# A retention and gated-MLP kernel: the first MLP layer of blocks 4 to 8 by seven block products, with part of the gated product on GpSimd

## The chip, the cores and the metric

The kernel runs on one core of a Trainium2 chip. The metric is the device time of one execution in microseconds, the median over several runs. The engines are named as in the profile: PE is TensorE (PEld its weight loads), DVE is VectorE, ACT is ScalarE, POOL is GpSimd, SP is SyncE, which issues most DMAs.

## What is computed

For 8 batches, 8 heads, 576 positions and head size 64 the reference computes a retention (attention with a decay in place of a softmax), puts the heads side by side to 4608 tokens of 512 numbers, and sends them through an MLP with 2048 hidden units and the gate h·cos(h):

```python
scores = scale * np.matmul(q, k.transpose(0, 1, 3, 2))
Dmat = np.where(rel >= 0, gamma[:, None, None] ** rel[None, :, :], 0.0)
attn = np.matmul(scores * Dmat[None], v)
x = attn.transpose(0, 2, 1, 3).reshape(B * S, H * D)
h = x @ w_in            # 4608x512 by 512x2048
g = h * np.cos(h)
out = g @ w_out         # 4608x2048 by 2048x512
```

## The kernel before

The tokens are cut into nine MLP blocks of 512 tokens (`NTB`, j = 0 to 8), and the retention into 18 units of 256 positions of one batch (two of them gather the last 64 positions of four batches each). Two units make the 512 tokens of one block.

A unit: SP loads k, q and v in float32 into staging buffers (L463); POOL casts k (L454) and scales q and v by powers of the decay (L496) into bf16; k and q are transposed, for the first two blocks by PE (L517), later by DMA (L532). PE computes the scores in 64x64 tiles (`scores`, L565, all its matmuls recorded on L563), DVE masks them (L599), PE computes the outputs (`outputs`, L637): a `main` phase inside the chunks, a `fill` phase that adds k times v to the running states in PSUM (`states`, L612), and a `cross` phase with the states of earlier chunks, which waits for the end of `main` (`after` [0]). ACT copies the states (L631) and the unit's output into `xt` (L710, recorded on L453). The running states have two PSUM banks, `ST[0]` and `ST[1]`, for even and odd batches.

The first layer (`mlp1`, L727) makes 16 hidden tiles of 128 units for a block: four matmuls (L737) accumulate in one PSUM bank, ACT takes sin(h + pi/2) into `cb` (L745), and DVE multiplies PSUM by `cb` into `gt` (L748). In blocks 0 to 2 a tile is made in two halves of 256 tokens, in blocks 3 to 8 at once for 512.

The second layer is plain for block 0 (`plain2`, L767). For blocks 1 to 8 (`wino2`, L805) it is cut in two along tokens, hidden units and output columns, and made of seven block products in place of eight: DVE forms sums of `gt` quarters into `s` (L823, L829), PE makes 7x16 matmuls of 128x256 (L862) that accumulate in three banks, ACT copies three intermediate results into `sn` (L453), DVE adds them to the banks into `os` (L874). The sums of the weights (`tw`) are made once (`wsums`, L787).

The order of the work is written by a planner (`Graph.run`, L204): each task has a fixed duration, a due time (a period of 28.8 us for each block) and buffers from small rotating pools (`POOLS`, L315): six PSUM banks `bk`, three staging buffers each of k, q, v, three `cb`, three `sn`, three `os`. It simulates the five engines, an exclusive use of one SBUF port by DVE and POOL tasks that are marked `port`, the DMA, and PE's instruction fetches in steps of 256 (`FETCH`), and writes each engine's queue in the order of the simulated starts. Every queue then runs in that fixed order and waits on semaphores. Short matmuls on ones (L401) fill PE's gaps in the first microseconds.

Of the kernel before, what the change touches and what calls it, by code (L numbers as in the profile page):

```python
# [6 lines left out]
ALU = mybir.AluOpType  # L7
AF = mybir.ActivationFunctionType
F32 = mybir.dt.float32
# [120 lines left out]
class Graph:  # L130
# [3 lines left out]
    AHEAD, FETCH = 2000, 3000  # L134
# [44 lines left out]

    def first(self, t):  # L180
        need = {}
        for b in t.allocs:
            need[b.pool] = need.get(b.pool, 0) + 1
        return all(b in self.fifo[b.pool][:need[b.pool]] for b in t.allocs if b.pool in self.fifo)
# [19 lines left out]
    def run(self, dma_rate):  # L204
# [3 lines left out]
        left = [256, self.FETCH]  # L208
# [21 lines left out]
        def pick(e):  # L230
            cand = []
            for t in ready[e]:
# [4 lines left out]
                if e == "pe" and t.count > left[0]:  # L237
                    s = max(s, left[1] - t.dur * left[0] / t.count)
# [22 lines left out]
        while n < len(self.tasks):  # L261
# [10 lines left out]
            e = t.eng  # L272
            ready[e].remove(t)
# [5 lines left out]
            if e == "pe":  # L279
                if t.count > left[0]:  # L280
                    left[1] = s + t.dur * left[0] / t.count + self.FETCH
                    left[0] += 256
                left[0] -= t.count
# [9 lines left out]
            if t.dma is not None:  # L293
                dma_free = max(dma_free, s + (1700 if e == "pool" else 1150)) + t.dma
                done = dma_free + t.tail
# [18 lines left out]
class Kernel:  # L314
    POOLS = dict(bk=6, stgk=3, stgv=3, stgq=3, natk=3, natv=3, qnat=2, kt=3, qt=3, pt=4, sba=3, sbb=3, sbr=8, xt=2,  # L315
                 gt=2, s=9, cb=3, os=3, sn=3)
# [3 lines left out]
                cb=(TB, BF16), os=(1024, F32), sn=(TB, F32))  # L320
    FORDER = [0, 1, 2, 3, 8, 9, 10, 11, 4, 5, 6, 7, 12, 13, 14, 15]
    SPLIT = 2
    PLAIN = (0,)
    NOXBAR = {0, 1}
    PERIOD, T0, T1 = 28800, 14000, 30000

    def __init__(self, nc, es, q, k, v, w_in, w_out, out):
# [8 lines left out]
        self.TW = {n: sb(f"tw{n}", [128, 8 * 256], BF16) for n in (1, 2, 4)}  # L336
        self.WV = sb("wv", [128, 40], F32)
# [10 lines left out]
        self.ST = [nc.alloc_psum_tensor(f"st{i}", [128, 512], F32) for i in range(2)]  # L348
# [26 lines left out]
    def emit(self, order):  # L375
# [4 lines left out]
        for t in order:  # L380
            if t.eng == "pe":
                gap = t.start - warm
                if gap > 400 and self.wb.left:
                    self.warm(int((gap - 300) / 110 if not warm else 0.6 * (gap - 150) / 57))
# [126 lines left out]
    def tpe(self, src, off, rk, dst, wk, eng):  # L511
        bk = Buf("bk")

        def mm(e):
            tb = self.at(bk).ap().bitcast(BF16)
            for c in range(4):
# [5 lines left out]
                 alloc=() if self.first else (self.wb,), name="tpe", count=9)  # L522
# [17 lines left out]
    def emit_lanes(self, name, prio, phases, alloc=()):  # L540

        parts, t, n = [], 200, 0
        for lanes, reads, writes, after in phases:
# [7 lines left out]
            n += 2 * len(order) + 1  # L551
# [60 lines left out]
    def states(self, u, s, lanes, reads, writes):  # L612
        nk, nv = self.tiles[u]["natk"], self.tiles[u]["natv"]
        x = u[0] % 2
        for r in range(2):
            for c in range(4):
                for y in range(2):
                    i, o = 512 * y + (2 * c + r) * D, 512 * y + self.head(c, r) * D
                    lanes[s, r].append((64, self.mm(
                        lambda r=r, c=c: ap(self.ST[x], 512, 64 * r, 64, c * 64, [1, 64]),  # L620
                        lambda i=i: ap(self.at(nk), 1024, 64 * s, 64, i, [1, D]),
                        lambda o=o: ap(self.at(nv), 1024, 64 * s, 64, o, [1, D]),
                        start=u[1] == s == c == y == 0)))
        reads += [(t, y) for t in (nk, nv) for y in range(2)]
        writes.append(("st", x))
# [5 lines left out]
    def snap(self, u, s):  # L631
        b = self.sbd[u, s] = Buf("sba" if s == 0 else "sbr" if u[1] else "sbb")
        x = u[0] % 2
        self.copy("act", 280, lambda: self.at(b).ap(), lambda: ap(self.ST[x], 512, 0, 128, 0, [1, 256]),
                  [("st", x)], [(b,)], late=1000 if s == 0 else 3000)

    def outputs(self, u, prio, late):  # L637
# [5 lines left out]
        main, fill, cross = ({q: [] for q in self.LANES} for _ in range(3))  # L643
# [37 lines left out]

        for s in range(2):
# [3 lines left out]
        for s in range(2):  # L686
            for p in range(2):
                inter(s, p, 1 - s, cross)
# [5 lines left out]
        phases = [(main, reads, writes, [])]  # L694
        if late:
            phases.append((fill, [], [], []))
            for v, s in late:
                self.states(v, s, *phases[-1][:3])
        phases.append((cross, reads, writes, [0]))
# [27 lines left out]
    def mlp1(self, j, f, ses, prio):  # L727
# [7 lines left out]
        def mm(e):  # L735
            for c in range(4):
# [7 lines left out]
                 w=[(bk,)], alloc=[gt] + [self.wb] * (j == 1 and f == 0), prio=prio, name=f"m1_{j}_{f}", count=9)  # L744
# [8 lines left out]
    def store(self, j, half, os, cols=(0, DM)):  # L753
        c0, cn = cols[0], cols[1] - cols[0]
        if j < 8:
# [3 lines left out]
        for p0, n, b, r, step in parts:  # L759
# [4 lines left out]
                r=[(os, c) for c in range(2) if cols[0] <= 256 * c < cols[1]],  # L764
                sem=lambda p0=p0: f"o{os.slot}_{p0}_{c0}", dma=1550 * cn / DM * n / 128)

    def plain2(self, j, base, span):  # L767
        gt = self.gt[j]
        for half in range(2):
            os = Buf("os")  # L770
            for tt in range(2):
                bk = Buf("bk")
                for qd in range(4):
                    def mm(e, tt=tt, qd=qd, bk=bk, half=half):
                        for f in range(4 * qd, 4 * qd + 4):
# [6 lines left out]
                             + [("wout", qd, 0), ("wout", qd, 1)], w=[(bk,)], prio=base + span * i / 16, name=f"p2_{j}", count=9)  # L782
                self.copy("act", 490, lambda os=os, tt=tt: ap(self.at(os), 1024, 0, 128, 512 * tt, [1, 512]),
                          lambda bk=bk: self.at(bk).ap(), [(bk,)], [(os, 0 if tt == 0 else 1)])
# [20 lines left out]
    def wino2(self, j, base, span):  # L805

        gt = self.gt[j]
        S_ = {(i, q): Buf("s") for i in range(1, 5) for q in range(2)}
# [16 lines left out]
        for q in range(2):  # L825
            for i, x, y, r, op in (
                    (3, lambda q=q: a(0, 0, q), lambda q=q: a(0, 1, q), ak(0, 0, q) + ak(0, 1, q), ALU.subtract),
                    (4, lambda q=q: a(1, 0, q), lambda q=q: sv(2, q), ak(1, 0, q) + [(S_[2, q],)], ALU.subtract)):
                self.one("dve", 610, lambda e, i=i, q=q, x=x, y=y, op=op: e.tensor_tensor(sv(i, q), x(), y(), op),  # L829
                         r=r, w=[(S_[i, q],)], port=True, name=f"S{i}_{j}")  # L830
        A, Bb, C = Buf("bk"), Buf("bk"), Buf("bk")
# [12 lines left out]
        def right_t(i):  # L844
# [7 lines left out]
            7: (left_s(3), right_b(0, 1), lambda q: [(S_[3, q],), ("wout", q, 1)], A, False),  # L852
# [3 lines left out]
        for n, p in enumerate((1, 2, 6, 5, 7, 3, 4)):  # L856
            l, rr, keys, bank, first = spec[p]
            for q in range(2):
                def mm(e, l=l, rr=rr, bank=bank, first=first, q=q):
                    for f in range(4 * q, 4 * q + 4):  # L860
                        for tt in range(2):
# [139 lines left out]
```

## Time and profile before

| what | value |
|---|---|
| runs of the kernel before | 300.94, 302.74, 304.18 us; median 302.74 |
| the profiled execution | 301.62 us, of them 299.9 us span (first to last instruction) |
| granted TensorE clock | 1.000 |
| PE busy from 90 to 210 us | 120.0 of 120 us |
| DVE, ACT, POOL busy from 150 to 180 us | 22.54, 17.05, 13.12 us |
| last matmuls end, last ACT instruction ends | 295.74, 296.36 us |
| share of the 16 DMA engines, 120 to 150 us, 210 to 240 us | 1.04, 0.13 |

The profile is of one execution. Busy time counts from an instruction's start to its end, so that two pipelined instructions overlap: an instruction's duration is longer than the distance of two starts. The chain of waits is followed back from the last instruction: each piece is released by the one before it, so that its shares say what the end waited for. In a group's line stand the count, the busy time, the mean duration and the idle time in front of it with its releaser.

### The profile page before, as it was taken

Reading aid. Unit: us, or ns where it says so; the run is one execution under the profiler, and the core shown is the slowest. Engines: PE = TensorE matmul, PEld = TensorE weight load, DVE = VectorE, ACT = ScalarE, POOL = GpSimd, SP = SyncE. Lnnn points to the kernel's source line nnn. Section 1 sums busy time; section 2 is a strip of 40 time slices with the busy share of each in tenths; the row PEclk is TensorE's granted clock in tenths of the full one; section 3 lists DMA queues with packets and bytes.
Section 4 is the critical chain, followed back from the end, with each engine's and each line's share of the span. In section 5 each row is a group of like instructions: output and inputs, shape, how many; then the busy total and the mean of one; then the engine's idle time right before and its main releaser. Section 6 shows DMA issues by size and latency. Waiting matters only on the chain.

```text
span 299.9 us, 9086 instructions
## 1 busy us (share of the span) xinstructions
PE 285.2 (95%) x3809; PEld 202.7 (68%) x3815; DVE 213.0 (71%) x379; ACT 169.7 (57%) x315; POOL 101.4 (34%) x125
## 2 busy tenths in 40 slices
PE   6789888999999999999999999999999999999994
PEld 6667665666788876766676667666766666666683
DVE  2776495659985889697868686959777666667721
ACT  5369876556667565645655565466565555545420
POOL 3821960665825614825363515172100000000000
PEclk9999999999999999999999999999999999999999
DMA  7999789999999799997999986892103000300115
GB/s 199 252 203 274 202 129 236 280 200 299 207 251 297 151 194 281 214 227 210 229 280 232 244 188 94 194 236 53 24 2 140 2 2 2 140 2 0 70 73 140
DMA packets 101640, 49.87 MB, mean 166 GB/s; under 512 B 43488, under 2 KB 97248, under 8 KB 101600
## 3 DMA queue, kind: packets, MB, share of 16 engines
q1 hardware_dynamic: 97376, 45.10, 63.6%
q0 software_dynamic: 4224, 4.19, 8.8%
q8 instruction: 30, 0.49, 0.7%
q14 instruction: 10, 0.08, 0.1%
HBM read 36.70 MB, written 9.44 MB: 154 GB/s over the span
## 4 chain that ended last, share of the span: by engine, by line
PE 78%; DMA 14%; POOL 5%; issue 1%; SPq 0%; ACT 0%; DVE 0%; DVEq 0%
PE bk L737 35%; PE bk L862 33%; DMA stgq<-in_q_dram 8%; PE bk L563 6%; DMA wout<-in_moe_w_out_dram 3%; DMA win<-in_moe_w_in_dram 3%; PE bk L776 2%; POOL qnat L496 2%; POOL natv L496 2%; PE st L563 1%; POOL natk L454 1%; SPq L463 0%; POOL win L717 0%; POOL wout L721 0%; DVE qnat L496 0%
## 5 line engine op out<-in xcount | busy, mean ns | idle before, releaser
L745 ACT ACTIVATE cb<-bk,cpi 128x256 bf16<-128x256 f32 (+1 forms) x192 | 108.3, 583 | 82.0 <-PE bk L737 79.9
L737 PE MATMUL bk<-xt,win 128*128 128x256 bf16 (+1 forms) x768 | 144.2, 326 | 1.0 <-DMA win<-in_moe_w_in_dram 0.7
L748 DVE TENSOR_TENSOR gt<-bk,cb 128x256 bf16<-128x256 f32 (+1 forms) x192 | 103.8, 555 | 54.9 <-ACT cb L745 47.8
L737 PEld LDWEIGHTS bk<-xt,win 128*128 128x128 bf16 x768 | 72.3, 98 | 39.7 <-DVE pt L599 1.4
L496 POOL TENSOR_TENSOR natv<-stgv,wv 128x512 bf16<-128x512 f32 x36 | 37.7, 1070 | 37.0 <-PE bk L563 20.6
L599 DVE TENSOR_TENSOR pt<-bk,tr 128x512 bf16<-128x512 f32 x68 | 42.7, 682 | 5.5 <-PE bk L563 5.4
L496 POOL TENSOR_TENSOR qnat<-stgq,wq 128x512 bf16<-128x512 f32 x32 | 35.0, 1112 | 15.9 <-DMA stgq<-in_q_dram 15.3
L454 POOL CAST natk<-stgk 128x512 bf16<-128x512 f32 x34 | 21.3, 653 | 55.8 <-DMA stgk<-in_k_dram 44.8
L862 PE MATMUL bk<-wout,gt 128*128 128x256 bf16 x256 | 32.7, 273 | 0.0
L862 PE MATMUL bk<-tw,s 128*128 128x256 bf16 x256 | 32.7, 273 | 0.0
L862 PE MATMUL bk<-wout,s 128*128 128x256 bf16 x256 | 32.4, 273 | 0.0
L862 PEld LDWEIGHTS bk<-tw,s 128*128 128x128 bf16 x256 | 24.9, 98 | 8.1
L862 PEld LDWEIGHTS bk<-wout,gt 128*128 128x128 bf16 x256 | 24.7, 98 | 6.4
L862 PEld LDWEIGHTS bk<-wout,s 128*128 128x128 bf16 x256 | 24.7, 98 | 6.1
L453 ACT ACTIVATE xt<-bk 128x512 bf16<-128x512 f32 x36 | 23.5, 728 | 0.5 <-PE bk L563 0.5
L874 DVE TENSOR_TENSOR os<-bk,sn 128x512 f32<-128x512 f32 x24 | 16.4, 683 | 10.4 <-PE bk L862 10.4
L453 ACT ACTIVATE sn<-bk 128x512 f32<-128x512 f32 x24 | 14.3, 597 | 13.8 <-PE bk L862 13.8
L862 PE MATMUL bk<-tw,gt 128*128 128x256 bf16 x128 | 16.4, 273 | 0.0
L776 PE MATMUL bk<-wout,gt 128*128 128x512 bf16 x58 | 15.3, 380 | 0.6 <-issue 0.3
L862 PEld LDWEIGHTS bk<-tw,gt 128*128 128x128 bf16 x128 | 12.5, 98 | 4.0
L829 DVE TENSOR_TENSOR s<-gt 128x1024 bf16<-128x1024 bf16 x16 | 12.8, 800 | 0.2
L563 PE MATMUL bk<-qt,kt 64*64 64x128 bf16 (+1 forms) x576 | 12.1, 217 | 0.4 <-ACT xt L453 0.4
(58 smaller groups left out, 187.7 us busy)
## 6 DMA issues: line engine op xcount, KB each, us to landing
stgk<-in_k_dram SPq DMA_DIRECT2D x16, 512.0 KB, 7.0
stgq<-in_q_dram SPq DMA_DIRECT2D x16, 512.0 KB, 6.9
stgv<-in_v_dram SPq DMA_DIRECT2D x16, 512.0 KB, 6.9
out_dram<-os SPq DMA_DIRECT2D x16, 512.0 KB, 3.3
win<-in_moe_w_in_dram POOLq DMA_DIRECT2D x4, 512.0 KB, 9.0
wout<-in_moe_w_out_dram POOLq DMA_DIRECT2D x4, 512.0 KB, 10.0
stgk<-in_k_dram SPq DMA_DIRECT2D x8, 128.0 KB, 3.4
stgq<-in_q_dram SPq DMA_DIRECT2D x8, 128.0 KB, 3.5
```

Of the source, the lines that this page charges most:

```text
L453: return self.one(eng, dur, lambda e: e.activation(dst(), src(), AF.Copy), r=r, w=w, **kw)
L454: return self.one(eng, dur, lambda e: e.tensor_copy(dst(), src()), r=r, w=w, port=True, **kw)
L496: self.one(eng, 610 if eng == "dve" else 1000, lambda e, out=out, inp=inp, tab=tab, col=col, hs=hs: e.tensor_tensor(out(), inp(), ap(tab, ...
L563: return lambda e: e.matmul(out(), lhs(), rhs(), start=start, stop=True, skip_group_check=True)
L599: self.one("dve", 610, lambda e, r=r, b=b, pt=pt: e.tensor_tensor(ap(self.at(pt), 1024, 0, 128, 512 * r, [64 * ny * ny, 8 // ny // ny], [1 ...
L737: inst = e.matmul(ap(self.at(bk), 512, 0, 128, 0, [1, n]), ap(self.WIN, 4 * DFF, 0, 128, c * DFF + 128 * f, [1, 128]), ap(self.at(xt), 204 ...
L745: self.one("act", 70 + n, lambda e: e.activation(ap(self.at(cb), TB, 0, 128, 0, [1, n]), ap(self.at(bk), 512, 0, 128, 0, [1, n]), AF.Sin, ...
L748: self.one("dve", 75 + n / 0.96, lambda e: e.tensor_tensor(ap(self.at(gt), NF * TB, 0, 128, f * TB + 256 * h0, [1, n]), ap(self.at(bk), 51 ...
L776: inst = e.matmul(self.at(bk).ap(), ap(self.at(gt), NF * TB, 0, 128, f * TB + 256 * half + 128 * tt, [1, 128]), ap(self.WOUT, NF * DM, 0, ...
L829: self.one("dve", 610, lambda e, i=i, q=q, x=x, y=y, op=op: e.tensor_tensor(sv(i, q), x(), y(), op), r=r, w=[(S_[i, q],)], port=True, name ...
L862: inst = e.matmul(ap(self.at(bank), 512, 0, 128, 256 * tt, [1, 256]), l(f, tt), rr(f), start=(first and f == 0 and tt == 0), stop=True, sk ...
L874: self.one("dve", 610, lambda e: e.tensor_tensor(view(h, c), ap(self.at(bank), 512, 0, 128, 0, [256, 2], [1, 256]), ap(self.at(sn[name]), ...
```

## The change

Blocks 4 to 8 get their first layer by `seven1`, which works like `wino2`: for each of four groups g (two tiles of either half of the hidden units) PE makes seven products of four 128x256 matmuls into three banks, 112 matmuls for a block where there were 64 of 128x512. ACT copies three intermediate results per group into `sn`; DVE adds them to the banks into a new float32 buffer `h`; ACT takes the sine from `h`; POOL multiplies `h` by `cb` into `gt`. For the fourth quarter of a group the sine and the product (on DVE) read PSUM as before. `xsums` makes four sums of `xt` on DVE for each block, `wsums1` eight sums of `w_in` once.

With it come other edits. Both running states lie in one bank, cleared by a DVE memset for each batch, and `bk` has seven banks; `outputs` is cut into five phases in which the two row halves of PE never write the same bank, with three waits of PE for its own earlier phases in place of one. Staging goes from three buffers to two, `pt` from four to two, `s` from nine to six (one sum overwrites `gt`), `os` from three to two, `cb` and `sn` grow to four and five. The planner's fetch model, its counts and a DMA delay are new. The `w_out` loads wait for q of unit (1,1) where they waited for v, and unit (2,0) for the third `w_out` load where it waited for the second. In the last block bank A and its copies and stores are split by token half.

In the order of the queues after the change, PE has 240 matmuls more; POOL has 60 products more, between its conversions; SP's order is the same up to its 42nd instruction, with waits for POOL in more places. On POOL the four `w_out` loads stand ahead of the conversion of q of unit (1,1), behind which they stood. Thirteen units are converted, or are first in POOL's queue, when its first gated product comes.

```diff
-    POOLS = dict(bk=6, stgk=3, stgv=3, stgq=3, natk=3, natv=3, qnat=2, kt=3, qt=3, pt=4, sba=3, sbb=3, sbr=8, xt=2,
-                 gt=2, s=9, cb=3, os=3, sn=3)
+    POOLS = dict(bk=7, stgk=2, stgv=2, stgq=2, natk=3, natv=3, qnat=2, kt=3, qt=3, pt=2, sba=3, sbb=3, sbr=8, xt=2,
+                 gt=2, s=6, cb=4, os=2, sn=5, xs=3, h=4)
-    AHEAD, FETCH = 2000, 3000
+    AHEAD, FETCH = 2000, 6500
-        self.ST = [nc.alloc_psum_tensor(f"st{i}", [128, 512], F32) for i in range(2)]
+        self.ST = nc.alloc_psum_tensor("st", [128, 512], F32)
...
+        if u[1] == s == 0:
+            self.one("dve", 340, lambda e: e.memset(ap(self.ST, 512, 0, 128, 256 * x, [1, 256]), 0.0), w=[("st",)])
...
-        phases = [(main, reads, writes, [])]
-        if late:
-            phases.append((fill, [], [], []))
-            for v, s in late:
-                self.states(v, s, *phases[-1][:3])
-        phases.append((cross, reads, writes, [0]))
+        for x, y, after in (
+                (cut(cross, 0, 0, 8), cut(late_lanes, 1, 0, 4), []),
+                (cut(main, 0, 0, 3), cut(late_lanes, 1, 4, 8), []),
+                (cut(main, 0, 3, 99), cut(main, 1, 0, 7), [0]),
+                (cut(late_lanes, 0, 0, 4), cut(main, 1, 7, 99), [1]),
+                (cut(late_lanes, 0, 4, 8), cut(cross, 1, 0, 8), [2])):
+            if any([*x.values(), *y.values()]):
+                phases.append(({**x, **y}, reads + state[0], writes + state[1], after))
...
+    def seven1(self, j, g, prio, span):
+        A, Bb, C = Buf("bk"), Buf("bk"), Buf("bk")
+        sn = {n: Buf("sn") for n in ("p1", "u2", "p5")}
...
+        spec = {
+            1: (left_w(0, 0), right_x(0, 0), self.xkeys(j, (0,)) + slabs(0), A, True),
+            2: (left_w(1, 0), right_x(1, 0), self.xkeys(j, (0,)) + slabs(0), Bb, True),
+            6: (left_t(2), right_s(2), [(X[2],)] + ts(2), A, False),
+            5: (left_t(1), right_s(1), [(X[1],)] + ts(1), C, True),
+            7: (left_w(0, 1), right_x(0, 1), [(xt, "s3")] + slabs(1), A, False),
+            3: (left_w(1, 1), right_s(4), [(X[4],)] + slabs(1), C, False),
+            4: (left_t(4), right_x(1, 1), self.xkeys(j, (1,)) + ts(4), A, False),
+        }
+        def snap(name, bank):
+            self.copy("act", 490, lambda: self.at(sn[name]).ap(), lambda: self.at(bank).ap(),
+                      [(bank,)], [(sn[name], x) for x in range(2)])
+        def gate(h, n, bank, name):
+            cb = Buf("cb")
...
+            if name:
+                src = Buf("h")
+                key = (src,)
+                self.one("dve", 610, lambda e: e.tensor_tensor(
+                    self.at(src).ap(), self.at(bank).ap(), self.at(sn[name]).ap(), ALU.add),
+                    r=[(bank,)] + [(sn[name], x) for x in range(2)], w=[key])
+            self.one("act", 580, lambda e: e.activation(
+                self.at(cb).ap(), self.at(src).ap(), AF.Sin, bias=self.CPI.ap(), scale=1.0), r=[key, ("cpi",)], w=[(cb,)])
+            eng = "pool" if name else "dve"
+            self.one(eng, 1050 if name else 610, lambda e: e.tensor_tensor(dst(), two(src), two(cb), ALU.mult),
+                     r=[key, (cb,)], w=[(gt, 8 * n + 2 * g + f, h) for f in range(2)], port=eng == "pool")
...
+            self.one("pe", 4 * 109, mm, r=keys, w=[(bank,)], alloc=[gt], prio=prio + span * n / 7, name=f"M{p}_{j}", count=8.4)
+            if p == 1:
+                snap("p1", A)
+            elif p == 2:
+                gate(0, 0, Bb, "p1")
+            elif p == 6:
+                snap("u2", A)
+            elif p == 5:
+                snap("p5", C)
+            elif p == 7:
+                gate(1, 1, A, "p5")
+            elif p == 3:
+                gate(0, 1, C, "u2")
+            else:
+                gate(1, 0, A, None)
...
-        gate = [(st["v", (1, 1)], 0)]
+        gate = [(st["q", (1, 1)], 0)]
-        self.unit((2, 0), gate=[("wout", 1, 0)])
+        self.unit((2, 0), gate=[("wout", 2, 0)])
...
+            if j + 1 >= self.SEVEN and not last:
+                self.xsums(j + 1)
+                for g in range(4):
+                    self.seven1(j + 1, g, base + PER * g / 4, PER / 4)
+            elif not last:
```

## The prediction

> **What bounds the kernel now.** I read the page first: busy time, slices, chain shares.
>
> ```profile
> PE 285.2 (95%) x3809; PEld 202.7 (68%) x3815; DVE 213.0 (71%) x379; ACT 169.7 (57%) x315; POOL 101.4 (34%) x125
> ...
> PE   6789888999999999999999999999999999999994
> ```
>
> PE is busy all the time from slice 8 on, that is from about 60 us; only the start has holes. Next the chain of waits in order of time. Its pieces run from one release to the next, so a piece divided by its count is the distance of two matmuls.
>
> ```profile
> 129.31 4.32 PE bk L737 x20
> ...
> 188.77 4.32 PE bk L737 x20
> ...
> 264.41 1.73 PE bk L737 x8
> ...
> 282.62 13.11 PE bk L862 x120
> ```
>
> A first-layer matmul of 512 columns takes 1.73/8 = 0.216 us, one of 256 columns 13.11/120 = 0.109 us. The first two lines are the same place two periods apart: a period is (188.77 - 129.31)/2 = 29.73 us, all of it PE. So a matmul's time taken out after 60 us comes off the end, as long as the others keep up. What they have left is in the table of stretches (PE, PEld, DVE, ACT, POOL, then clock, DMA share, GB/s):
>
> ```profile
> 150.00:180.00 30.00, 30.00 (x397) 20.03 (x396) 22.54 (x35) 17.05 (x30) 13.12 (x14) 1.00 1.00 236
> ...
> 210.00:240.00 30.00, 29.91 (x373) 19.65 (x371) 21.90 (x34) 16.34 (x27) 0.83 (x1) 1.00 0.13 42
> ```
>
> ACT has room, DVE little, POOL much; after 210 us POOL is done, while the last units are used at 236 and 251 us. The durations come from the groups by shape, the collisions and the waits from the timeline:
>
> ```profile
> L496 POOL TENSOR_TENSOR qnat<-stgq,wq 128x512 bf16<-128x512 f32 x32 | 35.0, 1112 | 15.9 <-DMA stgq<-in_q_dram 15.3 <-PE bk L862 0.4
> ...
> L874 DVE TENSOR_TENSOR os<-bk,sn 128x512 f32<-128x512 f32 x24 | 16.4, 683 | 10.4 <-PE bk L862 10.4
> ...
> L453 ACT ACTIVATE sn<-bk 128x512 f32<-128x512 f32 x24 | 14.3, 597 | 13.8 <-PE bk L862 13.8
> ```
>
> ```profile
> 157.02 2.48 DVE L599 TENSOR_TENSOR pt<-bk,tr 128x512 bf16<-128x512 f32 x4
> ```
>
> ```profile
> 208.34 2.49 POOL L496 TENSOR_TENSOR natv<-stgv,wv 128x512 bf16<-128x512 f32 x2 [6.20 <-PE bk L563]
> 208.58 1.35 DVE L829 TENSOR_TENSOR s<-gt 128x1024 bf16<-128x1024 bf16 x1
> ```
>
> ```profile
> 237.30 0.21 PEld L563 LDWEIGHTS bk<-qt,sbr 64*64 64x64 bf16 x16 [0.20 <-PE bk L563]
> ```
>
> DVE instructions in a row start (2.48 - 0.68)/3 = 0.60 us apart, though each lasts 0.68. At 208 us a DVE sum of two SBUF operands and a POOL product overlap, and both stretch: 1.35 us for the sum where others of L829 take 0.69, 2.49 for the POOL pair where others take 2.04. They exclude each other, for up to 0.66 us. The last fence is PE waiting for its own earlier phase in a unit with nothing between.
>
> **The change part by part.**
>
> *Products (path).* A block has 64 x 0.216 = 13.84 us of first layer and will have 112 x 0.109 = 12.24 us. That is -1.60 us a block, and -8.0 us for five. PE is the chain throughout these blocks, so all of it counts: a period goes from 29.73 to 28.13 us.
>
> *What the others must do in 28.13 us.* ACT: 17.05 of 30 us now is 16.9 a period; 12 copies of 0.597 add 7.2: 24.1 busy, 86%. DVE: the 16 gated products become 12 sums and 4 products of the same length (0.683 by L874 against 0.688 by L748). The 12 and 4, 8 masks, 8 sums for `s` and 3 for `os` are 35 instructions, at 0.60 21.0; the four sums of `xt` are half as long as L829's 1024 columns, between 0.35 and 0.60 each, together 1.9: 22.9 us. POOL: 12 products at 1.00 to 1.11 (rows of L496; the pair of 2.04 gives 1.0 a start), 12.6; a unit's conversion is four of these and two casts of 0.55 to 0.61, 5.1. The queue shows that when the first product comes only five units remain for four periods: 6.4 a period, 19.0 together. None exceeds 28.13, so the load itself costs nothing, covered by PE; without that cover DVE would be the next, at 22.9.
>
> *The exclusion.* 8 sums in `s` and 4 of `xt` a period meet a POOL that is busy two thirds of the time. Each can lose 0 to 0.66 us: 0 to 7.9 a period. DVE becomes the bound at (28.13 - 22.9)/12 = 0.43 us each. I take 0.33, half of the row, as POOL's instruction is met at any point: 26.9, still under PE, but with hardly any room.
>
> *A rule against this.* The Trainium skill (GPSIMD Engine Reference, 4.1 Engine selection) puts two-input elementwise work on VectorE, as GpSimd is about half as fast. In this trace the ratio is 1.04 to 1.11 against 0.60 to 0.69 us. By the rule the 12 products would stay on DVE, at 0.60 each 7.2 us more, 30.1 a period, and DVE would bound at 0.4 us over the period before; by the rows POOL's slowness costs nothing, as it has the time.
>
> *New waits inside a group (path).* Bank A holds product 1, is copied by ACT, takes product 6, is copied, takes product 7, is read by DVE, takes product 4. In PE's new queue mostly one second-layer piece (8 x 0.109 = 0.87) and one other product (0.44) lie between: 1.31 us. A copy needs the tail of the last matmul (its 0.27 less the 0.11 to the next), 0.597, and a handover between 0.02 and 0.2 us: 0.8 to 1.0. An ACT instruction in front (0.56 to 0.69) therefore costs PE 0 to 0.4, say 0.25. There are 3 copies in each of 20 groups, 60. Lower end: none meets one, 0 (the 24 copies of L453 now stop PE nowhere in the list of waits). Upper end: all, 15 us. Behind a waiting PE stands everything, behind a waiting ACT copy the sines. I take one in six, +2.5, near the lower end, since the row of 24 is the nearest, though with ACT at 57%.
>
> *Five phases (path).* Now one wait of PE for itself, with the state products (0.23 us) in front, does not show; uncovered it is 0.20 idle (last fence), some 0.28 from start to start. Two of the three new waits have three matmuls of 0.056, 0.17 us, in front: up to 0.06 each, 0.12 for each of 16 full units: 0 to +1.9. I take +1.2.
>
> *The end.* Last matmul 295.74, ACT 0.60, then two stores issued one after the other. After: a copy of half the width (the 128x256 copies of `sba` take 0.38), and one store left to issue (the last four take SP 2.96 us, 0.74 each): -0.2 and up to -0.7. I take -0.7, range -1.2 to 0.
>
> *The start.* PE waits for data before 60 us. The q conversion of unit (1,1), 2.0 us, moves behind the four `w_out` issues, 3.0 us on POOL: scores (1,1) up to 3 us later, `w_out` up to 2 us earlier; PE's queue puts a second-layer piece ahead of those scores. SP and POOL now wait for two staging buffers; SP's order is the same to instruction 42. A stall by fetching (the timeline has one of 1.04 us at 47 us) may move. Taken 0, range -2 to +3. Later staging has a lead: POOL ends 25 us or more before the last units. Stores stand behind loads that wait for POOL, and two `os` buffers come back a period later, so this is 0 too, up to 1 if that lead is gone.
>
> *Once.* Eight weight sums at 0.69, 5.5 us on DVE in the period before block 4, with 22.9 to 24: at most 29.5 against PE's 29.73, 0 to +1, taken 0. A memset per batch: off the path, 0.
>
> *Sum.* -8.0 + 2.5 + 1.2 - 0.7 = -5.0 on the profiled 301.62 (span 299.9 and 1.7 around it): 296.6. That execution is 1.1 under the median of the three runs, 302.74, which themselves lie 3.2 apart.
>
> **The rivals.** *All is hidden.* Copies and phases cost nothing and a fetch stall goes: 301.6 - 8.0 - 0.7 - 1.0 = 291.9. For it: PE has no wait for ACT's copies now. Against: ACT goes from 57 to 86%.
>
> *The shared port binds.* The 12 sums lose 0.58 each, and DVE's period is 22.9 + 7.0 = 29.9: four periods at +0.2, the last without unit work at -1.6, phases and end +0.5: 301.3; at the full 0.66, 30.8, it is 305. It decides from 0.43 us. For it: the 1.35 us row. Against: most sums of L829 now take 0.69.
>
> *Slower: the copies stop PE.* Each of the 60 copies finds one ACT instruction in front: 301.6 - 7.5 + 15 = 309. At 7.5/60 = 0.125 us each the gain is gone; at 0.175 it is slower by 1%. For it: the fixed order and three handovers in a row on bank A. Against: 1.31 us of other work.
>
> **How the numbers follow.** About 1%, 3 us, is what a measurement of this kernel tells from no change. Forecast 0.55, at 296.6 (its own range 293.5 to 299.5); all hidden 0.17; port 0.16; copies 0.12. The range 291.5 to 304 holds nearly all of the first, two thirds of the second, most of the third: 0.8. Faster by over 1% (under 299.7): 0.53 + 0.17 = 0.70; within: 0.02 + 0.16 = 0.18; slower: 0.12.
>
> **What would show it.** Right: L737 and its new line keep 0.109 a matmul; the periods of blocks 4 to 8 last 28 to 29 us, PE idle for ACT's copies under 4 us in all; each unit's outputs some 0.1 us longer; one short ACT copy last. Wrong: a list of waits in which PE waits over 8 us for `sn` or `h`; sums of `s` or `xs` at 1.2 us on the mean; holes of PE before 60 us changed by over 3 us.

## The result, and the profile after

The changed kernel takes 316.92 us at the median of four runs (315.19 to 320.35), against 302.48 us for the kernel before beside it: a ratio of 1.0457, 95% interval 1.0372 to 1.0542. It is slower, by 14.4 us where 6 us less was forecast. Executions more than 1.5% above the same kernel's fastest, which show a lower granted clock, are left out of the ratios, and where half or more of a kernel's executions were so, its range is given instead.

The page of the changed kernel, its busy time and slices:

```profile
PE 285.0 (91%) x4054; PEld 229.2 (73%) x4061; DVE 244.3 (78%) x416; ACT 195.8 (62%) x378; POOL 180.7 (57%) x185
...
PE   7759999997999999999999999799999999999930
PEclk9999999999899999999999999999999999999995
```

PE's row has a 7 from 71 to 79 us, another from 197 to 204 us, and next to nothing in the last 13 us of the span. The chain of waits, in order of time, is no longer all PE:

```profile
215.45 1.53 PE bk L1019 x15
216.98 1.15 DVE s L981
219.18 0.73 ACT cb L867
...
257.70 0.70 DVE h L864
258.43 0.73 ACT cb L867
...
289.24 12.34 PE bk L1019 x112
```

12.34/112 is 0.110 us: a matmul of 256 columns costs what it did. Between them stand DVE sums and sines, where the chain before had only PE. The table of stretches (PE, PEld, DVE, ACT, POOL, clock, DMA share, GB/s):

```profile
150.00:180.00 30.00, 29.68 (x456) 25.04 (x454) 27.67 (x43) 22.82 (x41) 24.31 (x24) 1.00 0.95 212
...
210.00:240.00 30.00, 29.11 (x434) 24.04 (x432) 27.34 (x39) 21.77 (x39) 24.63 (x21) 1.00 0.40 72
```

Four engines are now at 73 to 99%. The groups by shape and the list of waits name the pair that gets in each other's way, POOL's products and DVE's sums:

```profile
L870 POOL TENSOR_TENSOR gt<-h,cb 128x512 bf16<-128x512 f32 x60 | 75.0, 1261 | 38.1 <-ACT cb L867 37.3 <-DVE os L1039 0.6
...
L864 DVE TENSOR_TENSOR h<-bk,sn 128x512 f32<-128x512 f32 x60 | 39.7, 681 | 9.5 <-PE bk L879 5.7 <-ACT sn L464 3.0 <-issue 0.6
...
L981 DVE TENSOR_TENSOR s<-gt,s 128x1024 bf16<-128x1024 bf16 x16 | 17.3, 1094 | 0.0
...
L811 DVE TENSOR_TENSOR xs<-xt,xs 128x512 bf16<-128x512 bf16 x5 | 4.0, 800 | 0.0
```

In the kernel before, the same sum as in L981 has a mean of 742 ns:

```profile
L829 DVE TENSOR_TENSOR s<-gt,s 128x1024 bf16<-128x1024 bf16 x16 | 11.8, 742 | 0.2
```

The list of waits (in all, times, longest). A wait of the weight loads (PEld) runs beside one of PE, so the two do not add:

```profile
PEld bk L879 <- DVE h L864: 5.2, 7, 1.9
...
PE bk L879 <- DVE h L864: 3.0, 4, 1.6
...
PEld bk L879 <- ACT sn L464: 0.9, 3, 0.5
PE bk L879 <- ACT sn L464: 0.8, 2, 0.6
```

The budget, from the starts of all matmuls in both traces (a matmul's own time taken as 0.417 ns a column plus 2.2 ns, which gives the measured 109 and 215 ns; one of 64 rows counted as a quarter, since 32 of them with 128 columns follow each other within 0.57 us at 161 us; the matmuls on ones left out; the rest is lost time):

| where | us |
|---|---|
| PE's own work, 260.1 to 251.9 (0.2 of it a matmul whose record the second trace lacks) | -8.2 |
| waits outside the outputs between 150 and 270 us, 1.7 to 7.8 | +6.2 |
| outputs of 18 units, 16 x 0.22 + 2 x 0.24 | +4.0 |
| 60 to 90 us: a hole of 2.0 us and matmuls at half clock behind it | +3.4 |
| from PE's end to the end of the span, 4.2 to 13.0 | +8.9 |
| the rest | +0.4 |
| span, 299.9 to 314.6 | +14.7 |

**One of the waits.** The timeline around 200 us, DVE's queue and what stands behind it:

```profile
199.36 0.70 DVE L811 TENSOR_TENSOR xs<-xt 128x512 bf16<-128x512 bf16 x1
199.73 1.24 POOL L507 TENSOR_TENSOR qnat<-stgq,wq 128x512 bf16<-128x512 f32 x1
...
199.99 1.53 DVE L976 TENSOR_TENSOR s<-s,gt 128x1024 bf16<-128x1024 bf16 x1
...
201.27 1.26 POOL L870 TENSOR_TENSOR gt<-h,cb 128x512 bf16<-128x512 f32 x1 [0.29 <-ACT cb L867]
201.44 1.37 DVE L811 TENSOR_TENSOR xs<-xs,xt 128x512 bf16<-128x512 bf16 x1
...
202.73 1.27 DVE L864 TENSOR_TENSOR h<-bk,sn 128x512 f32<-128x512 f32 x2
...
203.47 0.61 PE L879 MATMUL bk<-xt,tx 128*128 128x256 bf16 x4 [1.58 <-DVE h L864]
```

Three DVE sums of two SBUF operands each meet a POOL product: 0.70, 1.53 and 1.37 us, where the undisturbed ones take 0.41 (`xs`) and 0.69 (`s`). That is 2.1 us more. Behind them in DVE's fixed queue stands the sum into `h` that empties bank A, and PE's product 4 waits 1.58 us for that bank. Of all 64 sums of `gt` quarters, 31 take over 0.75 us, where 13 did in the kernel before.

**The outputs.** PE's waits for its own earlier phase show in one unit, as distances between the lines of the timeline:

```profile
151.16 0.24 PE L574 MATMUL bk<-qt,sba 64*64 64x128 bf16 x2
...
151.42 0.19 PE L574 MATMUL st<-natv,natk 64*64 64x64 bf16 x1
151.56 0.47 PE L574 MATMUL bk<-pt,natv 64*64 64x128 bf16 x20
151.86 0.22 PE L574 MATMUL bk<-qt,sbb 64*64 64x128 bf16 x2
...
152.09 0.22 PE L574 MATMUL bk<-qt,sba 64*64 64x128 bf16 x2
152.22 0.22 PE L574 MATMUL st<-natv,natk 64*64 64x64 bf16 x2
...
152.46 0.61 PE L879 MATMUL bk<-xt,win 128*128 128x256 bf16 x4
```

A unit of the same size in the kernel before, its first line and the matmul that follows it:

```profile
162.42 0.64 PE L563 MATMUL bk<-pt,natv 64*64 64x128 bf16 x32
...
163.50 1.04 PE L737 MATMUL bk<-xt,win 128*128 128x512 bf16 x4
```

Ahead of the third and the fifth phase stand steps of 0.13 to 0.14 us, where neighbours start 0.01 to 0.06 apart; the wait ahead of the fourth, at 151.86, does not show. From its first start to the start of what follows, this unit takes 1.30 us, and the one before the change 1.08. Most units take 1.29 us with five phases, where they took 1.05 to 1.08 with three.

**The end.** The timeline and the table of stretches, from the last 14 us:

```profile
301.60 0.38 ACT L464 ACTIVATE os<-bk 128x256 f32<-128x256 f32 x1 [0.49 <-PE bk L1019]
301.93 4.01 SPq L904 DMA_DIRECT2D out_dram<-os  x2
```

The last ACT instruction of the kernel before, whose span ends at 299.9 us:

```profile
295.76 0.60 ACT L453 ACTIVATE os<-bk 128x512 f32<-128x512 f32 x1 [4.64 <-PE bk L862]
```

The stores after the change:

```profile
308.50:313.50 5.00, 0.00 (x0) 0.00 (x0) 0.00 (x0) 0.00 (x0) 0.00 (x0) 0.50 0.13 47
```

All engines are done at 302 us. Then stores move at 47 GB/s with a DMA share of 0.13, two engines of sixteen. (The clock of 0.50 there comes after PE's last matmul and slows none.) The Trainium skill (DMA: Bandwidth & Descriptors, Why a DMA increments its semaphore by 16 and not by 1) says that a DMA is spread over the largest number of engines, at most 16, that divides the slowest dimension of both sides; for the 2 of `[[S * DM, 2], [DM, 64], [1, cn]]` that would be two, and the trace agrees.

### The profile page after: what moved, and what is told of

Its sections match the earlier page's. It is cut to its first block, busy times and chain, and to the rows that moved or that the text cites. A ratio compares the mean times of both kernels' runs of the same rounds, so it can differ in the third digit from the quotient of the medians.

```text
span 314.6 us, 9726 instructions
## 1 busy us (share of the span) xinstructions
PE 285.0 (91%) x4054; PEld 229.2 (73%) x4061; DVE 244.3 (78%) x416; ACT 195.8 (62%) x378; POOL 180.7 (57%) x185
## 4 chain that ended last, share of the span: by engine, by line
PE 71%; DVE 10%; issue 5%; ACT 4%; DMA 4%; POOL 1%; SPq 0%; DVEq 0%; POOLq 0%
PE bk L1019 25%; PE bk L761 18%; PE bk L879 16%; PE bk L574 7%; PE bk L929 3%; DVE h L864 2%; DMA win<-in_moe_w_in_dram 2%; DMA stgq<-in_q_dram 2%; DVE pt L610 2%; ACT cb L867 2%; PE st L574 1%; DVE s L976 1%; DVE s L981 1%; DVE xs L811 1%; ACT sn L464 1%
## 5 line engine op out<-in xcount | busy, mean ns | idle before, releaser
L870 POOL TENSOR_TENSOR gt<-h,cb 128x512 bf16<-128x512 f32 x60 | 75.0, 1261 | 38.1 <-ACT cb L867 37.3
L769 ACT ACTIVATE cb<-bk,cpi 128x256 bf16<-128x256 f32 (+1 forms) x112 | 53.3, 521 | 31.7 <-PE bk L761 31.5
L761 PE MATMUL bk<-xt,win 128*128 128x256 bf16 (+1 forms) x448 | 66.0, 291 | 1.2 <-ACT xt L464 0.5
L772 DVE TENSOR_TENSOR gt<-bk,cb 128x256 bf16<-128x256 f32 (+1 forms) x112 | 48.6, 457 | 17.9 <-ACT cb L769 16.8
L464 ACT ACTIVATE sn<-bk 128x512 f32<-128x512 f32 (+1 forms) x86 | 48.2, 586 | 19.6 <-PE bk L879 11.2
L867 ACT ACTIVATE cb<-h,cpi 128x512 bf16<-128x512 f32 x60 | 42.7, 726 | 23.8 <-DVE h L864 23.6
L465 POOL CAST natk<-stgk 128x512 bf16<-128x512 f32 x34 | 21.5, 656 | 52.9 <-DMA stgk<-in_k_dram 42.8
L1019 PE MATMUL bk<-wout,gt 128*128 128x256 bf16 x384 | 49.2, 273 | 0.0
L864 DVE TENSOR_TENSOR h<-bk,sn 128x512 f32<-128x512 f32 x60 | 39.7, 681 | 9.5 <-PE bk L879 5.7
L879 PE MATMUL bk<-xt,win 128*128 128x256 bf16 x240 | 35.6, 273 | 0.0
L879 PEld LDWEIGHTS bk<-xt,win 128*128 128x128 bf16 x240 | 22.6, 98 | 3.1
L879 PE MATMUL bk<-xs,tx 128*128 128x256 bf16 x160 | 22.6, 273 | 0.8 <-DVE pt L610 0.5
```

Of the source, the lines that this page charges most:

```text
L464: return self.one(eng, dur, lambda e: e.activation(dst(), src(), AF.Copy), r=r, w=w, **kw)
L761: inst = e.matmul(ap(self.at(bk), 512, 0, 128, 0, [1, n]), ap(self.WIN, 4 * DFF, 0, 128, c * DFF + 128 * f, [1, 128]), ap(self.at(xt), 204 ...
L769: self.one("act", 70 + n, lambda e: e.activation(ap(self.at(cb), TB, 0, 128, 0, [1, n]), ap(self.at(bk), 512, 0, 128, 0, [1, n]), AF.Sin, ...
L772: self.one("dve", 75 + n / 0.96, lambda e: e.tensor_tensor(ap(self.at(gt), NF * TB, 0, 128, f * TB + 256 * h0, [1, n]), ap(self.at(bk), 51 ...
L864: self.one("dve", 610, lambda e: e.tensor_tensor(self.at(src).ap(), self.at(bank).ap(), self.at(sn[name]).ap(), ALU.add), r=[(bank,)] + [( ...
L867: self.one("act", 580, lambda e: e.activation(self.at(cb).ap(), self.at(src).ap(), AF.Sin, bias=self.CPI.ap(), scale=1.0), r=[key, ("cpi", ...
```

## The experiments

Each is timed against the kernel before on the same chip, whose median was 301.5 to 301.7 us throughout.

**The last stores, mended in the changed kernel** (`e1_stores`)

```diff
-            self.one("sp", 640, lambda e: e.dma_start(
-                bass.AP(self.out, ..., [[S * DM, 2], [DM, 64], [1, cn]]),
+            for b in range(2):
+                self.one("sp", 640, lambda e, b=b: e.dma_start(
+                    bass.AP(self.out, ..., [[DM, 64], [1, cn]]),
```

> The changed kernel, with each split store of the last block issued as two stores of 64 partitions (64 rows of 256 numbers, as before the change) in place of one store whose target is written as 2 x 64 rows. Theory (the form of the store): the 13.0 us from the last matmul's end region (301.5) to the end of the span (314.6) fall back to 4 to 5 us as before; 316.9 - 8.5 = 308 to 309 us. Rival (the end is long because the last stores queue behind the earlier stores of the block, whatever their form): two more stores to issue, 316 to 318 us.

Measured: 304.43 to 313.42 us, median 312.16. From PE's end to the end of the span it takes 5.5 us in place of 13.0: the tail is the form of the stores. It is still over the 4.2 us of the kernel before, so the end split in two gains nothing even with whole stores. The last stores now move on all sixteen DMA engines:

```profile
306.00:307.00 1.00, 0.00 (x0) 0.00 (x0) 0.00 (x0) 0.00 (x0) 0.00 (x0) 1.00 0.99 209
```

In the profiled execution (312.43 us) PE itself ended later than in the changed kernel's profile (305.2 against 301.6 us), after holes at 20.6, 42.8 and 79.4 us and stretches at half clock, of which one is:

```profile
23.50:28.50 5.00, 5.00 (x25) 3.59 (x24) 1.39 (x4) 3.11 (x7) 1.09 (x2) 0.50 1.17 296
```

**The form of the stores alone, in the kernel before** (`e16_split_stores`)

```diff
-                    self.store(j, 1, os[1], (256, 512))
-                    self.store(j, 1, os[1], (0, 256))
+                    for c0 in (256, 0):
+                        for tt in range(2):
...
+                                bass.AP(self.out, ..., [[S * DM, 2], [DM, 64], [1, 256]]),
```

> The kernel before with the form of its four last stores alone changed: two stores for each column half, each over the two batches outermost (2 x 64 partitions x 256 columns), as in the changed kernel; the queues of the other engines are the same. My theory: such a store of 128 KB moves at about 48 GB/s, 2.7 us each and one after the other, where the whole ones moved at 200 to 380 GB/s: the span ends 6 to 8.5 us later, 308 to 310 us. Rival: in the changed kernel the tail grew by what stood in SP's queue ahead of the stores, not by their form: 301.5 to 303 us.

Measured: 311.73 us, ratio 1.0299 [1.0243, 1.0354]. PE ends at 295.7 us as before; 13.6 us follow in place of 4.2. Its stretch after the last engine, again two of sixteen DMA engines:

```profile
301.50:307.50 6.00, 0.00 (x0) 0.00 (x0) 0.00 (x0) 0.00 (x0) 0.00 (x0) 0.50 0.13 39
```

The form of four small stores, nothing else changed, costs 10.0 us. That is shown from both sides.

**Without the seven products** (`e2_no_seven`)

```diff
-    SEVEN = 4
+    SEVEN = 99
```

> The changed kernel with the first layer of blocks 4 to 8 by four matmuls of 512 columns as before (no seven products, no gated product on GpSimd), all else as changed, the new stores included. Theory (the seven products save 8.0 us of PE and lose some 6 to 7 us of it again in waits for DVE's sums into h): 316.9 + 8.0 - 6.5 = 318 to 319 us, and the waits of PE for h are gone. Rival 1 (the seven products are what makes the change slower, by more than they save): under 314 us. Rival 2 (they lose nothing): 325 us.

Measured: 314.5 us, ratio 1.0435 [1.0376, 1.0494], while the whole change has 1.0457 [1.0372, 1.0542]. The time lies between the theory's 318 us and the first rival's 314. The five blocks of seven products bring no gain in this kernel. PE loses 1.7 us between 150 and 270 us here, as in the kernel before.

**A quarter of POOL's product, order unchanged** (`e3_gate_quarter`)

```diff
+            w = 64 if name else 256
-            dst = lambda: ap(self.at(gt), ..., [TB, 2], [1, 256])
+            dst = lambda: ap(self.at(gt), ..., [TB, 2], [1, w])
```

> The changed kernel with GpSimd's gated products cut to a quarter of their columns (64 of each 256; the rest of gt is left as it was, so part of the result is not computed), the queues' order unchanged. Theory (exclusion on the shared port: DVE's sums of two SBUF operands wait for GpSimd, so the sums into h come late and product 4 waits): the sums of s, gt and xs fall from 1.1 us on the mean to under 0.85, PE's waits for h from 5 us to under 2, the time by 3 to 5 us, to 312 to 314. Rival (the waits come from the handovers in a row on bank A, whatever GpSimd does): the waits and the time stay, 316 to 318.

Measured: 310.87 us, ratio 1.026 [1.0189, 1.0332], 6.1 us below the change and below the theory's 312 to 314. PE's stretches of its profile, and the group that corresponds to L981:

```profile
150.00:180.00 30.00, 30.00 (x483) 25.78 (x472) 25.93 (x42) 24.18 (x44) 16.93 (x26) 1.00 0.95 216
180.00:210.00 30.00, 30.00 (x455) 26.00 (x453) 25.23 (x42) 23.59 (x44) 16.66 (x24) 1.00 0.88 171
```

```profile
L984 DVE TENSOR_TENSOR s<-gt,s 128x1024 bf16<-128x1024 bf16 x16 | 14.0, 887 | 0.0
```

PE has no hole left in these stretches, the waits between 150 and 270 us fall from 7.8 to 1.9 us, POOL's product from 1.261 to 0.493 us, and the mean of the 64 sums from 1.01 to 0.82 us. In the changed kernel the waits come from POOL's time beside DVE's sums, not from the seven products' shape.

**Five phases and one state bank in the kernel before** (`e4_before_phases`), **and the phases with two banks** (`e8_phases_two_banks`), **and these with a memset** (`e15_memset_two_banks`)

```diff
-        phases = [(main, reads, writes, [])]
...
-        phases.append((cross, reads, writes, [0]))
+                (cut(cross, 0, 0, 8), cut(late_lanes, 1, 0, 4), []),
...
+                (cut(late_lanes, 0, 4, 8), cut(cross, 1, 0, 8), [2])):
```

> The kernel before with one part of the change alone: both running states in one bank, cleared by a memset, and the outputs in five phases with three waits. Theory (the waits of PE for its own phases cost 0.22 us in each of 16 full units and 0.24 in each of the two others, as 1.29 against 1.07 and 1.15 against 0.91 in the two profiles): 302.5 + 4.0 = 306 to 307 us. Rival (PE's outputs are longer only because of the work around them, or other engines hide it): 302 to 304 us.

> The kernel before with the five phases of the outputs alone: two state banks, no memset. The kernel before with the phases, one bank and the memset took 309.6 us. My theory: the phases alone cost 5 us of TensorE time and the memset with the shared bank the rest (the holes near 21 us and 76 us): 305 to 308 us. Rival 1: the phases are the whole of it, holes too: 309 to 311 us. Rival 2: the phases cost nothing by themselves, the shared bank and the memset do: 301 to 303 us.

> The kernel before with five phases, two state banks, and the states cleared by memsets instead of by the first matmul's start flag. With phases alone it took 307.5 us, with phases, memset and one shared bank 309.6 us and a hole of 2.8 us at the 348th matmul. If the memset makes the difference: 309 to 310 us, second load of TensorE's code later than 20.5 us, and a hole over 2 us at the 348th matmul. If the shared bank does: 306.5 to 308 us, second load at 19 to 20 us, and a hole under 1 us there.

Measured: 309.61 us, ratio 1.0239 [1.0188, 1.029]; 307.51 us, 1.0198 [1.013, 1.0266]; 307.16 us, 1.0147 [1.009, 1.0204]. In all three a unit takes 1.29 us, as in the changed kernel: 4.0 us of PE over 18 units. With the phases alone, with or without the memset, the time is 6.0 and 5.4 us longer, so 1.4 to 2.0 us come with the order around them. (An expectation below names 12.5 and 7.5 us lost by matmuls of 64 rows. Those sums leave out every wait over 0.2 us, so their difference of 5 us is not the price of the phases; the units show 4.0.) The memset adds nothing; the shared bank adds 2.1 to 2.5 us, near what the intervals can tell, and its profile alone has stretches at half clock (3.4 us from 24.0 us, 6.8 us from 78.6). In the five kernels with a stall of PE of 2.6 to 3.3 us near 21 us the states share one bank (in the sixth such kernel it is 1.1 us), and it stands right behind the 348th matmul. In the changed kernel, and in the DMA queues from 21 to 22 us:

```profile
20.81 0.22 PE L574 MATMUL bk<-qt,sba 64*64 64x128 bf16 x2
24.15 0.24 PE L574 MATMUL bk<-qt,sba 64*64 64x128 bf16 x2 [3.12 <-issue]
```

```profile
q8 instruction: 1, 0.02, 6.1%
```

The kernel with two banks, five phases and the memset, at the same matmul, and its DMA queues from 19 to 20 us:

```profile
20.38 0.72 PE L750 MATMUL bk<-xt,win 128*128 128x256 bf16 x5
21.76 1.49 PE L750 MATMUL bk<-xt,win 128*128 128x256 bf16 x12 [0.66 <-issue]
```

```profile
q8 instruction: 1, 0.02, 5.9%
```

"Issue" is PE waiting for its own code here: a load of 16 KB ends at 22.8 us in the one and at 20.4 us in the other, 1.3 to 1.4 us ahead of the next matmul, and 1.3 to 1.5 us ahead of it in all eight kernels with a stall there. With five phases PE comes to the 348th matmul at 20.3 to 22.3 us, with three at 21.8 to 22.6; and with one bank the load starts 7.7 to 8.7 us after the one before it, with two 6.2 to 6.9. Why the load is later is open.

**Two banks, three phases, six rotating banks in the changed kernel, stores mended** (`e5_two_banks`)

```diff
-    POOLS = dict(bk=7, ...
+    POOLS = dict(bk=6, ...
-        self.ST = nc.alloc_psum_tensor("st", [128, 512], F32)
+        self.ST = [nc.alloc_psum_tensor(f"st{i}", [128, 512], F32) for i in range(2)]
```

> The changed kernel with its last stores whole in two parts of 64 partitions each (as in the run before), and with the states in two banks, the outputs' matmuls in the three phases of the kernel before and six rotating banks instead of seven. My theory: the five phases cost about 5 us on TensorE (the excess time of 64-row matmuls is 12.5 us in every kernel with one state bank and 7.5 us in the kernel before), and they also feed the holes near 20 us and 75 us after which the clock is granted at half; this kernel then takes 298 to 301 us, and the excess of the 64-row matmuls is 7 to 8 us. Rival 1: the phases cost little, the waits for VectorE's sums are all there is: 303 to 306 us. Rival 2: six rotating banks are too few for groups that hold three: 306 us or more, with TensorE waiting for banks in the blocks with seven products.

Measured: 311.45 us, ratio 1.0312 [1.026, 1.0365]. A unit's outputs are back at 1.05 us and the stall at 21 us is gone, as expected, but the time is not: PE has holes near 57, 74, 94 and 145 us of 1.3 to 2.0 us, and three of 1.1 to 1.4 us from 177 us on. The time is that of the second rival, six rotating banks. My theory lacked a term, which the next runs looked for in the planner.

**The seven products alone** (`e9_seven_only`), **planned with a longer product** (`e10_seven_1300`), **and that with a quarter of it** (`e14_quarter`)

```diff
-            self.one(eng, 1050 if name else 610, lambda e: e.tensor_tensor(dst(), two(src), two(cb), ALU.mult),
+            self.one(eng, 1300 if name else 610, lambda e: e.tensor_tensor(dst(), two(src), two(cb), ALU.mult),
```

> The kernel before with the seven products of the first layer alone (blocks 4 to 8, gated product on GpSimd), with the smaller buffers that they need room for; two state banks, three phases, six rotating banks, the stores of the end and the planner's model of the kernel before. My theory: 8.1 us of TensorE work fall away and about 6 us of waits for VectorE's sums come in their place, with nothing else to pay: 299 to 301 us. Rival 1: the waits came from the rest of the change (phases, order): 293 to 296 us. Rival 2: smaller buffers and the holes cost as much as in the whole change: 303 us or more.

> As the kernel with the seven products alone, but the planner is told that GpSimd's gated product takes 1.30 us instead of 1.05 us (1.26 us measured), which changes only the order of the instructions. If the waits for VectorE's sums come from an order that is planned too tight: 2 to 4 us below that kernel. If they come from the load that the mutual exclusion of VectorE and GpSimd puts on VectorE, whatever the order: within 1 us of it.

> Seven products alone in blocks 4 to 8, product planned at 1.30 us, with GpSimd's product over a quarter of its columns, the order unchanged; the gated activations of the other columns are left uncomputed. The same kernel with whole products took 302 to 305 us. If GpSimd's time beside VectorE's sums is what eats the gain: 294 to 298 us. If the waits are VectorE's and ScalarE's own work: 301 us or more.

Measured: 304.91 to 312.71 us; 303.95 us, ratio 1.0072 [1.0032, 1.0112]; 302.21 us, ratio 0.9982 [0.9938, 1.0027]. With only the smaller buffers and the order of the weight loads that go with them, the seven products take 8 us off PE's work and still end above the kernel before. A duration in the planner nearer to the measured one is worth 1 to 3 us (PE ends at 299.0 and 296.1 us in the two profiles). A quarter of POOL's product gains about 2 us here, not the 6 of the changed kernel, though the mean sums of `gt` quarters shorten too, from 0.90 to 0.99 us to 0.78 to 0.82: the second reading holds, and other waits are left. PE's list from 150 us on in the run with a quarter:

```profile
PE bk L1001 <- ACT sn L455: 1.6, 1, 1.6
PE bk L1001 <- DVE pt L601: 1.2, 2, 0.6
PE bk L860 <- ACT sn L455: 0.5, 1, 0.5
```

So what the exclusion costs in the changed kernel isn't what eats the gain here. Six rotating banks, of which a group of seven products holds three, could be why; no run here changes their number alone, and it is not shown.

**The planner's new model alone** (`e11_planner_only`), **and without the new delay** (`e18_fetch_only`)

```diff
-                dma_free = max(dma_free, s + (1700 if e == "pool" else 1150)) + t.dma
+                dma_free = max(dma_free, s + (2400 if e == "pool" and s > dma_free - 700 else 1700 if e == "pool" else 1150)) + t.dma
```

> The kernel before with the changed planner's model alone (the due times of code loads with 6500 in place of 3000, the counts, 2400 for a late load issued by GpSimd); only the order of the instructions differs. The whole change with whole stores, two state banks and three phases took 311.5 us, and the seven products alone, with the old planner, 304.9 to 305.3 us where they ran undisturbed. If the new model's order is what lies between them: 304 to 308 us, with holes of TensorE of 1 to 2 us near 30, 57, 74 and 94 us. If it is harmless and the difference comes from something else (the split end, seven products in another order): 301 to 302.5 us.

> The kernel before with the new model of code loads (due times with 6500, and the counts) but the old delay for loads that GpSimd issues. The whole new planner model took 306.5 us, with only the order of the instructions changed. If the model of the code loads is what costs: 305 to 307 us. If it is the longer delay of GpSimd's loads: 301 to 303 us.

Measured: 306.52 us, ratio 1.0148 [1.0063, 1.0232]; 302.06 us, ratio 1.0002 [0.9971, 1.0032]. The model of code loads is harmless; one constant, the delay of a late load by POOL, costs 4.5 us through the order alone. Its trace loses them in small holes from 60 us on (one of 1.7 us at 74.6), not in one place. So the planner can be the term that was missing in the run with two banks and three phases. This is its price in the kernel before; the next run tells of the changed kernel.

**The changed kernel with the old planner, stores mended** (`e12_old_planner`)

```diff
-    AHEAD, FETCH = 2000, 6500
+    AHEAD, FETCH = 2000, 3000
...
-                dma_free = max(dma_free, s + (2400 if e == "pool" and s > dma_free - 700 else 1700 if e == "pool" else 1150)) + t.dma
+                dma_free = max(dma_free, s + (1700 if e == "pool" else 1150)) + t.dma
```

> The changed kernel with whole stores and the old planner's model; seven products, one state bank, five phases and seven rotating banks stay. My theory adds up terms: 301.5 us of the kernel before, less 8.1 for the products, plus 5 for the phases, 6 for the waits for VectorE's sums, 1.2 for eight small stores instead of four: 305 to 306 us. Rival, that the holes near 20 us and 75 us come with one state bank and its memset whatever the planner: 309 us or more.

Measured: 311.2 us, ratio 1.029 [1.0218, 1.0361]; the sum of terms missed by 5 to 6 us. It has stalls of 2.6 us behind the 348th matmul and 2.5 us at 40.8 us, and a granted clock of 0.50 from 24 to 27 and from 44 to 51 us. The rival holds: the stall comes with the shared bank, whichever planner. And the old planner shows no gain here: with the new one and the same mended stores the kernel took 304.43 to 313.42 us.

**Seven products where POOL is nearly free** (`e13_seven_from_6`)

```diff
-    SEVEN = 4
+    SEVEN = 6
```

> Seven products alone (states, phases, stores and planner of the kernel before, product planned at 1.30 us), but in blocks 6 to 8 only, where GpSimd has no more keys, queries and values to prepare. My theory (the waits come where GpSimd's own preparation and its products share the time with VectorE's sums): 3 times 1.6 us fall away and 1 to 2.5 us of waits are left: 298.5 to 300 us, the first version below the kernel before. Rival (each block with seven products costs as much in waits as it gives): 301 to 303 us.

Measured: 300.16 us, ratio 0.9933 [0.9893, 0.9973], with the states, phases, stores and planner of the kernel before and the product planned at 1.30 us. Two of its stretches:

```profile
180.00:210.00 30.00, 29.44 (x411) 21.19 (x410) 23.72 (x40) 16.92 (x29) 13.21 (x16) 1.00 0.73 149
210.00:240.00 30.00, 29.66 (x435) 25.44 (x433) 27.05 (x40) 23.49 (x44) 19.04 (x16) 1.00 0.15 46
```

It is the only version clearly below the kernel before, by 0.7%: three blocks take about 5 us off PE's work, and 1.6 to 2.0 us of that reach the time. The waits between 150 and 270 us rise by 2.9 us (1.7 to 4.6); the smaller buffers were not tried alone.

## Why the prediction was wrong

- *Products, -8.0.* Right: -8.2, or -8.0 with the missing record. L879 keeps 0.109 us a matmul.
- *What the others must do.* Nearly right for DVE (26.9 of 28.13 us forecast, 25 to 28 of 30 measured). POOL's product was taken from the rows of L496 at 1.00 to 1.11 us; it takes 1.261: 1.16 in the 24 products that meet none of DVE's sums of two SBUF operands, 1.33 in the 36 that do, so it too waits for DVE. POOL works 24 to 25 of 30 us, not 19 of 28.
- *The exclusion.* The size was right: the four groups of sums of `gt` quarters have means of 0.97 to 1.09 us, about 0.32 over 0.69, and I took 0.33. (Over the kernel before it is 0.26, as its means were 0.73 to 0.80.) The step from it failed. I compared a period's load with PE's and called the rest cover. But the sums come in rows, and they stand in DVE's fixed queue ahead of the sum that empties bank A. PE stops for the row, whatever room the period has (1.58 us in the row above).
- *New waits inside a group, +2.5.* The place was right and the size within the range, at +6.2; the releaser was not. ACT's copies stop PE 0.8 us, DVE's `h` sums 3.0 us (0.9 and 5.2 in the weight loads beside them). The rival that had the shared port bind from 0.43 us of loss was the right mechanism with a wrong point: it cost PE at 0.32.
- *Five phases, +1.2, 0 to +1.9.* Too small by a factor of three: 4.0 us in the units, 5.4 to 6.0 us in the time. I took the three matmuls in front for cover of all but 0.06 us of each of two waits. They cover less: two of the three waits show steps of 0.13 to 0.14 us, where neighbours start 0.01 to 0.06 apart, and that makes most of a unit's 0.22 to 0.24.
- *The end, -0.7.* The step that failed most: +8.9. I took SP's issue time (0.74 us a store) for the price of a store and did not look at its shape. ACT's last copy is 0.38 us as forecast, and then stores over two batches follow on two DMA engines at 47 GB/s. The form of these stores alone costs 10.0 us in the kernel before.
- *The start, 0.* PE has done the same work at 60 us (35.9 us in both), though with a new stall of 3.3 us for its code. Behind it, 3.4 us are lost between 60 and 90 us, where PE waits for DVE's masking late in a row of stretched sums, and then runs at half clock.
- *Not priced at all.* The planner's constants. They issue no instruction, and I treated them as a description. They change the order, and one of them alone costs 4.5 us in the kernel before. In the changed kernel the old ones show no gain, so how much of its time is theirs is open.

The two rivals that saw a loss both stayed inside the blocks of seven products. What decided lay outside: 8.9 us in the last stores, 4 to 6 in the phases. The parts' costs, each alone in the kernel before (stores 10.0, phases 5.4 to 6.0, shared bank about 2, planner 4.8, products 2 to 4), sum to 24 to 27 us and the whole change costs 14.4: they do not add. How they overlap is not resolved.

## What to carry to other kernels

Price every store by its shape, not by its issue: the outermost dimension decided whether the last stores moved on two DMA engines (share 0.13) or on all (0.99). When two engines exclude each other, ask what stands behind the stretched instruction in its fixed queue, not whether the period still has room. And cost an edit to a planner as an edit to the kernel: run the order alone.

## What was unexpected of the hardware

- *The clock.* A hole of PE of 2.0 to 3.3 us is at times followed, 2 to 3.5 us after its start, by a stretch of 3.4 or 6.8 us at a granted clock of 0.50, in which matmuls of 256 columns start 213 ns apart: after 6 of 13 such holes in these traces, and after two shorter ones (1.4 and 1.7 us). The Trainium skill (TensorE: Matmul & The Clock Gate, What's actually happening) has the clock at half after an idle window of about 3.4 us. All of these holes were shorter, so here the traces decide: less idle time can be enough. Why the other seven had no such stretch is open.
- *Code loads.* A stall by code keeps its place in the program (behind the 348th matmul in eight kernels of different order), but its length does not: 0.7 to 3.3 us, with the time at which PE gets there and at which the load ends.
